# All low words of the expert weights on VectorE, and one buffer moved from the low words to the raw weights

## The chip, the cores and the metric

The kernel runs on one core of a Trainium2 chip. The metric is the device time of one execution in microseconds (us). Engines are named as in the profile: PE is the matrix engine, PEld its weight loads, DVE the vector engine, ACT the scalar engine, POOL is GpSimd, SP issues most of the DMAs. Each engine works through its own instructions in order and waits on semaphores for the others.

## What is computed

Attention with a sigmoid in place of the softmax, then a mixture of eight experts in which every token goes to one expert (greedily, by the largest gate values, 224 tokens to each expert), then a two-layer network on all tokens. Inputs and outputs are fp32.

```
attn = 1 / (1 + exp(-(q @ k.T / sqrt(64) - log(448))));  x = attn @ v      # 4 x 12 heads, 448 rows
for e in range(8):                                        # tokens assigned to e: 224 of 1792
    h = maximum(x[mask] @ w1[e], 0)                       # 768 -> 1024
    out[mask] = h @ w2[e]                                 # 1024 -> 768
r = maximum(out @ w_in, 0);  g = s * (r * r) + b          # 768 -> 2048
y = g @ w_out                                             # 2048 -> 768
```

## The kernel before

**Two words for each operand.** Every fp32 operand of a matmul is split in two: a high word `wh`, which ACT makes by a copy that rounds to fp32r (`w_high`, line 242), and a low word `wl`, the raw value minus the high word (`w_low`, line 252). A product is then three passes: high by high, high by low, low by high. In `half_mm` (lines 713 and 714) the two passes with the high weights are one matmul, with the high and the low half of the moving operand side by side (448 columns), and the third is a matmul of 224 columns with `wl`. `short_mm` (lines 731 to 733) does the same in three matmuls.

**Units.** Weights come in units of 128 x 768 words (384 KB). A unit is loaded into a buffer `raw` by a DMA on SP's queue (`w_dma`, line 218), ACT makes `wh` from it, DVE or POOL makes `wl`, and then the `raw` buffer is free for a later DMA. There are four `raw`, five `wh` and five `wl` buffers. SP issues the next load as soon as a `raw` buffer is free. The list `where` tells which low words POOL makes: of the 16 units of an expert, numbers 0, 2, 4, 6 and 12 (in expert 0 only 6 and 12), 37 in all. All other low words are DVE's. Four more, of the first units, are made on POOL at the end of the attention by `w_low(G)`, in both kernels.

**An expert** (`expert`) has two loops. The first has eight column groups, one unit each: six by `half_mm`, two by `short_mm`. After each, ACT copies half of the PSUM result (line 718), DVE adds it to the other half (line 719), and the result is rounded into `u` (ACT line 780, DVE line 781, or 736 behind `short_mm`). The second loop has six column groups `d` of eight 128-row blocks, so that each group uses one unit and a third; its results go into `y` (ACT 725, DVE 726) in experts 0 to 5, and into the operands of the mixing stage in experts 6 and 7 (DVE 823, 828, 835, 768, 770). In experts 0, 2, 4, 5 and 6 `x_split` brings in the next expert's rows during the first loop: three transposes on PE (704), a copy on ACT (706), a subtraction on DVE (707), four times.

**What sets the order.** All orders are written out by hand. `advance` is called inside `half_mm`, right behind the addition on line 719, and queues what the next units need: loads up to 8 units ahead, low words up to `use + ahead - 1`, high words up to `use + ahead`, where `use` is the number of units handed to PE so far and `ahead` is 5.

**The stages**, by the profile's clock: attention to about 165 us, the assignment of tokens to 204, experts 0 and 1 to 270, the first layer for them (`layer_in`) to 331, experts 2 and 3 to 396, `layer_in`, the second layer (`outputs`) to 544, experts 4 to 7 to 680, then the first layer in a form with seven half-size products in place of eight (`layer_mixed`), and `outputs` again. `outputs` scatters finished rows to DRAM by indirect DMAs on POOL's queue (`scatter`, line 853); the rows of an expert are fetched by two indirect DMAs on the same queue (`gather`, line 609).

Of the kernel before, what the change touches and what calls it, by code (L numbers as in the profile page):

```python
# [28 lines left out]
KD = DM // 128  # L29
KF = F1 // 128  # L30
# [33 lines left out]
def tile_kernel(ctx, tc, qT, kT, v, wg, w1, w2, wi, wo, s2, b2, cst, out):  # L64
# [1 line left out]
    V, A, G, T = nc.vector, nc.scalar, nc.gpsimd, nc.tensor  # L66

    const = ctx.enter_context(tc.tile_pool(name="const", bufs=1))
    wraw = ctx.enter_context(tc.tile_pool(name="wraw", bufs=4))
    wsp = ctx.enter_context(tc.tile_pool(name="wsp", bufs=5))  # L70
    wlp = ctx.enter_context(tc.tile_pool(name="wlp", bufs=5))
    xrp = ctx.enter_context(tc.tile_pool(name="xrp", bufs=2))
    dpool = ctx.enter_context(tc.tile_pool(name="dpool", bufs=1, space=DRAM))
    ctx.enter_context(tc.manual_schedule())
# [102 lines left out]
    units, where = [], []  # L177
    raws, splits, sums = {}, {}, {}
    nu = {"dma": 0, "pre": 0, "high": 0, "low": 0, "use": 0, "ahead": 5}
# [14 lines left out]
    for g in range(4):  # L194
        for e in (2 * g, 2 * g + 1):
            units += [w1[e, f] for f in range(KF)] + [w2[e, n] for n in range(KF)]
            where += [n in ((0, 2, 4, 6, 12) if e else (6, 12)) for n in range(2 * KF)]
        more = [narrow[f] for f in range(KG)] if g < 2 else []
        if g == 3:
            more = [(0, 1), (1, 1), (0, 2), (1, 2), (0, 3), (1, 3), (0, 4)]  # L200
            for f in range(2, KG // 2):
                more += [(f, 1), (f - 1, 4), (f, 2), (f, 3)]
            more += [(KG // 2 - 1, 4)]
        if g % 2:
            more += [w for of in products for w in of]
        units += more
        where += [False] * len(more)
# [38 lines left out]
    def w_low(eng=None):  # L246
        i = nu["low"]
        if i < nu["high"]:
            r, h = w_source(i), splits[i]
            lo = wlp.tile([128, KD, 128], F32R, name="wl")[:, :r.shape[1]]  # L250
            eng = eng or (G if where[i] else V)
            eng.tensor_sub(lo, r, h.bitcast(F32))  # L252
            splits[i] = (h, lo)
            nu["low"] += 1
# [304 lines left out]
    def full(pk):  # L559
        V.tensor_copy(flag, pk)  # L560
# [42 lines left out]
    def gather(e):  # L603
        if e >= E:
            return
        for h, n in enumerate(HT):
            if (e, h) not in xr:
                xr[e, h] = xrp.tile([128, DM], F32, name="xr")
            G.indirect_dma_start(out=xr[e, h][:n], out_offset=None, in_=xs,
                                 in_offset=bass.IndirectOffsetOnAxis(ap=idx[:n, h, e:e + 1], axis=0))  # L610
# [69 lines left out]
    def row_ids():  # L680
        def put(dst, rows, h, col, r0, n, src):
            for r in range(0, n, 32):
                G.tensor_copy(dst[rows + r:rows + r + 32, col], idx[r0 + r:r0 + r + 32, h, src])

        a, b = slice(0, E, 2), slice(1, E, 2)
        put(idt[:, 0], 0, 0, slice(0, 4), 64, 64, a)
        put(idt[:, 0], 64, 1, slice(0, 4), 0, 64, a)
        put(idt[:, 1], 0, 1, slice(0, 4), 64, 32, a)
        put(idt[:, 1], 32, 0, slice(0, 4), 0, 96, b)
        put(idt[:, 2], 0, 0, slice(0, 4), 96, 32, b)  # L690
        put(idt[:, 2], 32, 1, slice(0, 4), 0, 96, b)
        put(idl, 0, 0, slice(0, 2), 0, 64, slice(0, 4, 2))
        put(idl, 64, 0, slice(0, 2), 0, 64, slice(4, E, 2))
# [15 lines left out]
    def half_mm(weights, src, n, done, ahead, tt=None):  # L709
        p = ps_m.tile([128, 512], F32, name="acc")  # L710
        for k in range(n):
            wh, wl = weights(k)
            T.matmul(p[:, :2 * CAP], wh, src[:, k].rearrange("p a s -> p (a s)"), start=(k == 0), stop=False)  # L713
            T.matmul(p[:, :CAP], wl, src[:, k, 0], start=False, stop=(k == n - 1))  # L714
        t2 = pool["y"].tile([128, 2, CAP], F32, name="tmp", bufs=pool["tmp"])
        bs = t2[:, 0]
        tt = t2[:, 1] if tt is None else tt
        A.copy(bs, p[:, CAP:2 * CAP])  # L718
        V.tensor_add(tt, p[:, :CAP], bs)
        if ahead:  # L720
            advance()
        done(tt, bs)

    def two(dst, src):
# [13 lines left out]
    def w_dmas():  # L738
        while nu["dma"] < min(nu["use"] + 8, len(units)):
            w_dma()  # L740

    def w_lows():
        while nu["low"] < min(nu["use"] + nu["ahead"] - 1, nu["high"]):
            w_low()

    def w_highs():
# [2 lines left out]
                w_pre()  # L749
            w_high()  # L750

    def advance():
        w_dmas()
        w_lows()
        while nu["pre"] < min(nu["use"] + nu["ahead"] + 1, nu["dma"]):
            w_pre()
        w_highs()
# [16 lines left out]
    def expert(e, y):  # L774
        x = xg.pop(e)
        u = ml.tile([128, KF, 2, CAP], F32R, name="u")

        def first(f):
            def done(tt, _):
                A.activation(u[:, f, 0], tt, AF.Relu)  # L780
                V.scalar_tensor_tensor(u[:, f, 1], tt, 0.0, u[:, f, 0].bitcast(F32), op0=ALU.max, op1=ALU.subtract)  # L781

            return done

        for f in range(KF):
            wh, wl = w_get()
            if f < KF - 2:
                half_mm(lambda k: (wh[:, k], wl[:, k]), x, KD, first(f), f < KF - 3)
                if f == KF - 3:
                    advance()  # L790
            else:
                short_mm(wh, wl, x, KD, (u[:, f, 0], u[:, f, 1]))
                if f == KF - 2:
                    advance()
            if 1 <= f <= 4 and (e % 2 == 0 or e == 5):
                x_split(e + 1, f - 1)
            if f >= 1 and out_rows:
                scatter(*out_rows.pop(0))
        if e in (4, 5):
            gather(e + 2)  # L800
        sl = slice((e % 2) * CAP, (e % 2 + 1) * CAP)
        held = []
        if e == 6:
            mov["b22"] = m2p.tile([128, HK, 2, S], F32R, name="x")
        elif e == 7:
            mov["t3"] = m2p.tile([128, HK, 2, S], F32R, name="x")

        def halves(name, d, cols=sl):
            return mov[name][:, d, 0, cols], mov[name][:, d, 1, cols]

        for d in range(KD):
            def second(k):
                n, c = divmod(d * KF + k, KD)
                if n == len(held):
                    held.append(w_get())
                return [w[:, c] for w in held[n]]

            def done(tt, spare):
                if e < 6:
                    two((y[:, d, 0, sl], y[:, d, 1, sl]), tt)  # L820
                    return
                if d < HK:
                    V.tensor_sub(spare, tt, full(0, d, sl))
                    work = [(halves("t1", d), spare)]
                    if e == 7:
                        work.append((halves("t3", d, slice(0, CAP)), full(1, d, slice(0, CAP))))
                else:
                    V.tensor_sub(full(1, d - HK, sl), full(1, d - HK, sl), tt)
                    work = [(halves("b22", d - HK), tt)]
                    if e == 7:  # L830
                        work.append((halves("t3", d - HK), full(1, d - HK, sl)))
                for dst, src in work:
                    A.copy(dst[0], src)
                for dst, src in pending:
                    V.tensor_sub(dst[1], src, dst[0].bitcast(F32))
                pending[:] = work
                if e == 7 and d in (0, 1):
                    mix(2 - d, slice(0, CAP))

            tt = None  # L840
            if e in (4, 5):
                tt = full(d // HK * 2, d % HK, sl)
            elif e > 5 and d < HK:
                tt = full(1, d, sl)
            half_mm(second, u, KF, done, d < KD - 1, tt)
            if not e and d == 1:
                row_ids()
            if e == 1 and 2 <= d <= 4:
                late_do(f"a{d - 2}", 0)

# [111 lines left out]
    def ahead(st, n, more=()):  # L962
        def lows():
            while na["low"] < min(n + 3, na["high"]):
                a_low(st)

        def sums():
            while na["sum"] < min(n + 5, 28):
                a_sum(st)

        w_dmas()
        work, more = [w_lows, lows, sums], list(more)
        while work or more:
            for q in (work, more):
                if q:
                    q.pop(0)()
        w_highs()
        while na["high"] < min(n + 4, 28):
            a_high(st)
# [261 lines left out]
```

## Time and profile before

| | before |
|---|---|
| median of 3 runs | 916.81 us (915.82 to 917.8) |
| the profiled execution | 918.23 us |
| its span, first to last instruction | 916.4 us |
| mean granted clock of PE | 0.976 of full speed |
| busy share: PE, DVE, ACT, POOL | 96%, 72%, 57%, 14% |

The profile is of one execution. A busy PE is one with a matmul in its pipeline, not one at its peak. An idle engine costs nothing unless PE waits for it in the end.

### The profile page before, as it was taken

The numbers are of one execution on the slowest core, as the hardware profiler recorded it, in microseconds if no ns is written. First come the engines' busy times: TensorE is split into PE (matmuls) and PEld (weight loads), VectorE is DVE, ScalarE is ACT, GpSimd is POOL, SyncE is SP. The second block draws the span as 40 slices with busy tenths as digits, with TensorE's granted clock in tenths as the row PEclk, the third lists the DMA queues.
The fourth block names the chain that finished last, engine by engine and source line by source line (L and its number), as shares of the span: only waits on it lengthen the run. The fifth ranks groups of instructions, "written<-read, shape, count | busy, mean of one in ns | idle before, by whom it ended". The sixth has DMA issues, their size and how long they took to land.

```text
span 916.4 us, 14216 instructions
## 1 busy us (share of the span) xinstructions
PE 879.4 (96%) x5219; PEld 755.4 (82%) x5219; DVE 659.4 (72%) x1101; ACT 519.5 (57%) x895; POOL 130.0 (14%) x131
## 2 busy tenths in 40 slices
PE   9999999789999999999999999899997999999997
PEld 4554555559989989999999998898996899999997
DVE  3877885646678777689767855877897788768680
ACT  6666666736555565643565545666655455654540
POOL 1000003222600033300000035422300000000003
PEclk9999999769999999999999999999998999999999
DMA  9989994755768775759643438665541212332213
GB/s 291 332 289 350 313 325 163 214 168 164 220 210 287 246 253 177 228 178 324 218 141 123 128 123 278 201 206 174 193 138 52 69 53 69 104 120 94 97 35 138
DMA packets 70186, 171.52 MB, mean 187 GB/s; under 512 B 8160, under 2 KB 25056, under 8 KB 70112
## 3 DMA queue, kind: packets, MB, share of 16 engines
q1 hardware_dynamic: 67840, 159.56, 53.3%
q0 software_dynamic: 2272, 11.01, 3.4%
q8 instruction: 42, 0.69, 0.3%
q14 instruction: 32, 0.26, 0.1%
HBM read 142.23 MB, written 28.31 MB: 186 GB/s over the span
## 4 chain that ended last, share of the span: by engine, by line
PE 52%; DVE 9%; DMA 7%; issue 5%; ACT 3%; POOL 1%; POOLq 0%; ACTq 0%; DVEq 0%; SPq 0%
DMA raw<-in_w_dram 7%; PE acc L1014 6%; PE acc L1016 6%; PE acc L1017 6%; PE acc L860 4%; PE acc L861 4%; PE acc L862 4%; PE acc L713 4%; DVE wl L252 4%; PE acc L1108 3%; PE acc L1106 3%; PE acc L1107 3%; PE acc L714 2%; ACT wh L242 1%; DVE u L781 1%
## 5 line engine op out<-in xcount | busy, mean ns | idle before, releaser
L242 ACT CAST wh<-raw 128x768 fp32r<-128x768 f32 (+1 forms) x240 | 195.5, 823 | 119.5 <-issue 48.0
L252 DVE TENSOR_TENSOR wl<-raw,wh 128x768 fp32r<-128x768 f32 (+1 forms) x199 | 191.9, 971 | 45.4 <-ACT wh L242 45.0
L252 POOL TENSOR_TENSOR wl<-raw,wh 128x768 fp32r<-128x768 f32 x41 | 82.5, 2016 | 439.9 <-ACT wh L242 439.8
L713 PE MATMUL acc<-u,wh 128*128 128x448 f32 x384 | 122.9, 378 | 1.6 <-DVE u L736 1.3
L714 PE MATMUL acc<-u,wl 128*128 128x224 f32 x384 | 102.3, 266 | 2.5 <-DVE wl L252 2.5
L302 ACT ACTIVATE attn<-psc,nls 112x896 f32<-112x896 f32 x96 | 88.8, 1008 | 10.1 <-PE psc L300 10.1
L713 PE MATMUL acc<-x,wh 128*128 128x448 f32 x288 | 93.7, 380 | 0.6 <-issue 0.6
L713 PEld LDWEIGHTS acc<-u,wh 128*128 128x128 f32 x384 | 72.8, 189 | 8.4 <-DVE u L736 3.0
L714 PE MATMUL acc<-x,wl 128*128 128x224 f32 x288 | 76.6, 266 | 2.3 <-DVE wl L252 2.3
L311 PE MATMUL pv<-attn,vt 112*64 112x448 f32 x384 | 77.5, 546 | 0.0
L714 PEld LDWEIGHTS acc<-u,wl 128*128 128x128 f32 x384 | 74.1, 193 | 2.8 <-DVE wl L252 2.8
L860 PE MATMUL acc<-y,wh 128*128 128x448 f32 x192 | 71.2, 371 | 0.9 <-ACT y L725 0.9
L861 PE MATMUL acc<-y,wh 128*128 128x448 f32 x192 | 70.6, 368 | 0.0
L862 PE MATMUL acc<-y,wl 128*128 128x448 f32 x192 | 70.3, 366 | 0.0
L311 PEld LDWEIGHTS pv<-attn,vt 112*64 112x64 f32 x384 | 25.4, 136 | 43.0 <-issue 36.1
L714 PEld LDWEIGHTS acc<-x,wl 128*128 128x128 f32 x288 | 55.0, 191 | 3.4 <-DVE wl L252 3.4
L713 PEld LDWEIGHTS acc<-x,wh 128*128 128x128 f32 x288 | 54.1, 188 | 4.5 <-issue 0.8
L1014 PE MATMUL acc<-wh,as 128*128 128x384 f32 x168 | 56.3, 335 | 0.0
L1017 PE MATMUL acc<-wh,as 128*128 128x384 f32 x168 | 56.2, 334 | 0.0
L1016 PE MATMUL acc<-wl,as 128*128 128x384 f32 x168 | 56.1, 334 | 0.0
L718 ACT COPY tmp<-acc 128x224 f32<-128x224 f32 x96 | 32.6, 340 | 21.1 <-PE acc L714 20.4
L781 DVE SCALAR_TENSOR_TENSOR u<-tmp,u 128x224 fp32r<-128x224 f32 x48 | 30.6, 639 | 18.0 <-ACT u L780 18.0
(341 smaller groups left out, 2027.9 us busy)
## 6 DMA issues: line engine op xcount, KB each, us to landing
raw<-in_w_dram SPq DMA_DIRECT2D x128, 384.0 KB, 3.5
raw<-nw SPq DMA_DIRECT2D x72, 384.0 KB, 3.2
craw<-in_wi_dram SPq DMA_DIRECT2D x16, 768.0 KB, 6.1
raw<-mx SPq DMA_DIRECT2D x32, 384.0 KB, 2.9
nw<-co SPq DMA_DIRECT2D x24, 384.0 KB, 6.9
craw<-in_wo_dram SPq DMA_DIRECT2D x8, 768.0 KB, 5.6
ra<-in_wo_dram SPq DMA_DIRECT2D x8, 768.0 KB, 6.4
rqk<-in_kT_dram SPq DMA_DIRECT2D x24, 224.0 KB, 6.6
```

The lines of the kernel that those rows point to most:

```text
L242: A.copy(h, r)
L252: eng.tensor_sub(lo, r, h.bitcast(F32))
L302: A.activation(attn[n][:, :, c, :], p[:, :, :S], AF.Sigmoid, bias=nls[:CP], scale=1.0 / math.sqrt(D))
L311: T.matmul(pv[j * 64:(j + 1) * 64, :S], v[:, c, j * D:(j + 1) * D], a[:, j, c, :], start=(c == 0), stop=(c == NC - 1))
L713: T.matmul(p[:, :2 * CAP], wh, src[:, k].rearrange("p a s -> p (a s)"), start=(k == 0), stop=False)
L714: T.matmul(p[:, :CAP], wl, src[:, k, 0], start=False, stop=(k == n - 1))
L860: T.matmul(p, wh, src[:, k, 0], start=first, stop=False)
L861: T.matmul(p, wh, src[:, k, 1], start=False, stop=False)
L862: T.matmul(p, wl, src[:, k, 0], start=False, stop=last)
L1014: T.matmul(acc, hi, wh[:, cols], start=(opens[j] and u == 0 and c == 0), stop=False, skip_group_check=True)
L1016: T.matmul(acc, hi, wl[:, cols], start=False, stop=False, skip_group_check=True)
L1017: T.matmul(acc, lo, wh[:, cols], start=False, stop=(u == 3 and c == 1), skip_group_check=True)
```

## The change

The list `where` is all False, so every low word that POOL made is DVE's. `raw` has five buffers in place of four, `wl` four in place of five. Since a half-used unit holds its `wl` buffer in the second loop of an expert, low words are queued there one unit less far ahead (`w_lows(2)`: up to `use + ahead - 2`), as in `outputs`; elsewhere the distance is as before. The call that fetches the rows of expert 6 is moved from behind expert 4's first loop to behind the third group of its second.

```diff
-    wraw = ctx.enter_context(tc.tile_pool(name="wraw", bufs=4))
+    wraw = ctx.enter_context(tc.tile_pool(name="wraw", bufs=5))
-    wlp = ctx.enter_context(tc.tile_pool(name="wlp", bufs=5))
+    wlp = ctx.enter_context(tc.tile_pool(name="wlp", bufs=4))
...
-            where += [n in ((0, 2, 4, 6, 12) if e else (6, 12)) for n in range(2 * KF)]
+            where += [False] * (2 * KF)
...
         if ahead:
-            advance()
+            advance(ahead)
...
-    def w_lows():
-        while nu["low"] < min(nu["use"] + nu["ahead"] - 1, nu["high"]):
+    def w_lows(n=1):
+        while nu["low"] < min(nu["use"] + nu["ahead"] - n, nu["high"]):
...
-    def advance():
+    def advance(n=1):
         w_dmas()
-        w_lows()
+        w_lows(n)
...
-                half_mm(lambda k: (wh[:, k], wl[:, k]), x, KD, first(f), f < KF - 3)
+                half_mm(lambda k: (wh[:, k], wl[:, k]), x, KD, first(f), int(f < KF - 3))
...
-        if e in (4, 5):
-            gather(e + 2)
+        if e == 5:
+            gather(7)
...
-            half_mm(second, u, KF, done, d < KD - 1, tt)
+            half_mm(second, u, KF, done, 2 if d < KD - 1 else 0, tt)
...
+            if e == 4 and d == 2:
+                gather(6)
...
-        work, more = [w_lows, lows, sums], list(more)
+        work, more = [lambda: w_lows(2), lows, sums], list(more)
```

Three places show how the instructions stand. On DVE, where expert 0 passes into expert 1 (719 is the addition behind a group, 252 a low word, 726 ends a group of the second loop, 781 one of the first), before:

```order
L719 TENSOR_TENSOR tmp<-acc,tmp 128x224
L726 TENSOR_TENSOR y<-tmp,y 128x224
L719 TENSOR_TENSOR tmp<-acc,tmp 128x224
L252 TENSOR_TENSOR wl<-raw,wh 128x768
L781 SCALAR_TENSOR_TENSOR u<-tmp,u 128x224
L719 TENSOR_TENSOR tmp<-acc,tmp 128x224
L252 TENSOR_TENSOR wl<-raw,wh 128x768
L781 SCALAR_TENSOR_TENSOR u<-tmp,u 128x224
```

and in the changed kernel:

```order
L719 TENSOR_TENSOR tmp<-acc,tmp 128x224
L726 TENSOR_TENSOR y<-tmp,y 128x224
L719 TENSOR_TENSOR tmp<-acc,tmp 128x224
L252 TENSOR_TENSOR wl<-raw,wh 128x768 x2
L781 SCALAR_TENSOR_TENSOR u<-tmp,u 128x224
L719 TENSOR_TENSOR tmp<-acc,tmp 128x224
L252 TENSOR_TENSOR wl<-raw,wh 128x768 x2
L781 SCALAR_TENSOR_TENSOR u<-tmp,u 128x224
```

Behind each of the first two groups of an expert DVE now has two low words, the first of which is for the third group. On DVE, at the start of the mixing stage (1077 and 770 prepare moving operands, 1122 and 1123 finish the second product, `wl<-xr` is the low word of a unit that is a sum of two), before:

```order
L719 TENSOR_TENSOR tmp<-acc,tmp 128x224
L252 TENSOR_TENSOR wl<-raw,wh 128x768
L252 TENSOR_TENSOR wl<-xr,wh 128x768
L231 TENSOR_TENSOR raw<-raw 128x384
...
L770 TENSOR_TENSOR rb<-rb,ra 128x3x224
L1077 TENSOR_TENSOR u<-ra,u 128x3x448
L1122 TENSOR_TENSOR tmp<-acc,tmp 128x448
L1123 SCALAR_TENSOR_TENSOR tmp<-tmp 128x448
L252 TENSOR_TENSOR wl<-xr,wh 128x768
```

and in the changed kernel, whose lines from here on are numbered two higher:

```order
L719 TENSOR_TENSOR tmp<-acc,tmp 128x224
L252 TENSOR_TENSOR wl<-raw,wh 128x768
L231 TENSOR_TENSOR raw<-raw 128x384
...
L770 TENSOR_TENSOR rb<-rb,ra 128x3x224
L1079 TENSOR_TENSOR u<-ra,u 128x3x448
L252 TENSOR_TENSOR wl<-xr,wh 128x768
L1124 TENSOR_TENSOR tmp<-acc,tmp 128x448
L1125 SCALAR_TENSOR_TENSOR tmp<-tmp 128x448
L252 TENSOR_TENSOR wl<-xr,wh 128x768
```

The low word of the first sum, for the fifth product, has moved from ahead of the whole preparation to behind it. On POOL, from the last scatter of the first `outputs` to the first of the second, before:

```order
L853 DMA out_dram<-rb,idt 1792x768
L609 DMA xr<-xs,idx 128x768
L609 DMA xr<-xs,idx 96x768
L252 TENSOR_TENSOR wl<-raw,wh 128x768 x5
L609 DMA xr<-xs,idx 128x768
L609 DMA xr<-xs,idx 96x768
L252 TENSOR_TENSOR wl<-raw,wh 128x768 x11
```

and in the changed kernel:

```order
L855 DMA out_dram<-rb,idt 1792x768
L609 DMA xr<-xs,idx 128x768
L609 DMA xr<-xs,idx 96x768
L609 DMA xr<-xs,idx 128x768
L609 DMA xr<-xs,idx 96x768
```

The two fetches for expert 6 stand right behind the scatters in both; only the low words are gone. The order on PE, ACT and SP is unchanged.

## Rows read from the trace of the kernel before

**Rows 1.** The page's groups, line 252: count | busy us, mean ns | idle before
```profile
L252 DVE TENSOR_TENSOR wl<-raw,wh 128x768 fp32r<-128x768 f32 (+1 forms) x199 | 191.9, 971 | 45.4 <-ACT wh L242 45.0
L252 POOL TENSOR_TENSOR wl<-raw,wh 128x768 fp32r<-128x768 f32 x41 | 82.5, 2016 | 439.9 <-ACT wh L242 439.8
```
**Rows 2.** Windows, experts 0 to 7: length, busy PE, PEld, DVE, ACT, POOL, clock, DMA
```profile
204.55:237.14 32.59, 32.04 (x217) 30.32 (x217) 21.33 (x38) 20.33 (x43) 13.88 (x22) 1.00 0.58 181
237.14:269.76 32.62, 31.58 (x207) 29.30 (x205) 24.00 (x42) 19.94 (x42) 9.08 (x6) 1.00 0.70 223
331.14:363.48 32.34, 32.01 (x218) 30.20 (x216) 22.26 (x37) 20.59 (x44) 8.51 (x6) 1.00 0.68 219
363.48:396.40 32.92, 31.39 (x206) 29.22 (x205) 23.41 (x40) 20.07 (x44) 9.83 (x6) 1.00 0.67 214
544.37:580.05 35.68, 33.16 (x217) 31.58 (x217) 20.12 (x35) 20.20 (x43) 18.30 (x19) 0.95 0.72 236
580.05:614.44 34.39, 32.01 (x218) 30.30 (x217) 27.21 (x42) 22.27 (x47) 13.63 (x8) 1.00 0.65 208
614.44:648.06 33.62, 31.75 (x219) 30.30 (x217) 27.13 (x45) 19.51 (x43) 8.63 (x5) 1.00 0.59 183
648.06:680.05 31.99, 30.87 (x206) 29.14 (x205) 27.75 (x48) 20.43 (x45) 8.22 (x5) 1.00 0.59 192
```
**Rows 3.** Timeline of PE in expert 0's first loop: start us, us, instruction
```profile
205.24 0.38 PE L713 MATMUL acc<-x,wh 128*128 128x448 f32 x1
...
205.87 0.37 PE L713 MATMUL acc<-x,wh 128*128 128x448 f32 x1
...
218.08 0.27 PE L731 MATMUL acc<-x,wh 128*128 128x224 f32 x1
...
219.09 0.27 PE L731 MATMUL acc<-x,wh 128*128 128x224 f32 x1
```
**Rows 4.** Waits of PE, 204 to 700 us: us in total, times, longest
```profile
PE acc L1108 <- DVE wl L252: 5.2, 1, 5.2
PE acc L714 <- DVE wl L252: 4.8, 4, 2.5
PE px L704 <- DVE x L707: 4.4, 4, 1.9
```
**Rows 5.** Timeline of DVE and POOL at 209, 243 and 622 us
```profile
209.43 3.46 DVE L252 TENSOR_TENSOR wl<-raw,wh 128x768 fp32r<-128x768 f32 x2
...
243.79 0.38 DVE L719 TENSOR_TENSOR tmp<-acc,tmp 128x224 f32<-128x224 f32 x1
...
622.07 1.82 POOL L252 TENSOR_TENSOR wl<-raw,wh 128x768 fp32r<-128x768 f32 x1 [1.71 <-ACT wh L242]
622.31 1.82 DVE L781 SCALAR_TENSOR_TENSOR u<-tmp,u 128x224 fp32r<-128x224 f32 x1 [0.54 <-ACT u L780]
```
**Rows 6.** Line 781 alone: duration ns min/median/max, first and last start
```profile
L781 DVE SCALAR_TENSOR_TENSOR u<-tmp,u x48: 376/392/2037, 208.8 to 664.2; 128x224 fp32r<-128x224 f32 x48
```
**Rows 7.** Timeline of DVE, POOL and ACT between 532 and 571 us
```profile
532.56 0.55 DVE L1031 TENSOR_TENSOR rb<-acc,rb 128x384 f32<-128x384 f32 x1
...
547.90 1.23 POOL L853 DMA_INDIRECT out_dram<-ra,idt  x1 [0.17 <-issue]
...
570.39 0.83 ACT L242 CAST wh<-raw 128x768 fp32r<-128x768 f32 x1 [2.94 <-DMA raw<-in_w_dram]
```
**Rows 8.** Timeline of DVE from expert 7's second loop into the mixing stage
```profile
669.33 2.04 DVE L823 TENSOR_TENSOR tmp<-ra 128x224 f32<-128x224 f32 x1
...
690.12 1.56 DVE L1077 TENSOR_TENSOR u<-ra,u 128x1344 fp32r<-128x1344 f32 x1
693.49 0.62 DVE L1122 TENSOR_TENSOR tmp<-acc,tmp 128x448 f32<-128x448 f32 x1 [1.81 <-ACT tmp L1113]
...
694.69 0.95 DVE L252 TENSOR_TENSOR wl<-xr,wh 128x768 fp32r<-128x768 f32 x1
```
**Rows 9.** Window at the start of the mixing stage, columns as in rows 2
```profile
692.20:699.00 6.80, 3.30 (x9) 2.96 (x10) 4.80 (x8) 4.10 (x7) 0.00 (x0) 0.50 0.00 0
```

## The prediction, made before the changed kernel was run

> **What bounds the kernel now.** I read the busy shares in the table first: PE is busy for 96% of the span, DVE for 72%. So the change can give back only what PE loses to waits. Which stages lose is seen in the windows of the eight experts, the stages for whose weights POOL makes low words [rows 2]. What an expert would take without waits follows from the spacing of the matmuls: two pairs of half_mm start 0.63 us apart, so a pair costs 0.315 us, and nine short matmuls take 1.01 us, so one costs 0.112 [rows 3]. An expert has 6 x 6 + 6 x 8 = 84 pairs and 36 short ones: 26.5 + 4.0 = 30.5 us. The windows with about 218 matmuls where the others have 206 hold twelve transposes more; at an estimated 0.09 us each, somewhat under the wider short ones, these take 1.1 us, so 31.6 us. Against that the windows lose, experts 0 to 7: 1.0, 2.1, 0.7, 2.4, 4.1, 2.8, 2.0 and 1.5 us, together 16.6 us. Then comes the start of the mixing stage, where PE waits once for 5.2 us.
>
> Next, what PE waits for [rows 4]: low words from DVE, and transposed rows (x, line 707) from DVE. Yet DVE is busy for only 56 to 87% of these windows [rows 2]. The timeline tells why [rows 5]: at 622.07 POOL starts a low word, 1.82 us long; 0.24 us later DVE starts line 781, which has 224 columns and a median of 0.392 us [rows 6], and takes 1.82 us. It is released as POOL ends. Every DVE instruction from 200 to 680 us that takes well over its own usual time runs beside a POOL low word: 31 of them, the first in the pair at 209.43 (3.46 us for two) [rows 5], the last at 669.33 (2.04 us for 224 columns, which take 0.38 elsewhere [rows 5]) [rows 8]; their excess sums to 39.2 us. Line 719, which takes one input from PSUM, is not among them. So a POOL low word does not relieve DVE; it holds it, and with it the ACT and PE work behind it in order.
>
> The Trainium skill speaks for and against the edit here (Perfetto Trace Analysis, section Optimizing Scalar/DVE Operations): with DVE saturated, offloading even to GPSIMD may make sense, but as the two share a read port it might not help. The 1.82 us of line 781 [rows 5] agree with the second half. By the first half alone, the added low words would come on top of DVE's busy time.
>
> **The change part by part.** *Low words to DVE.* Added: 37 at 0.97 us, the mean on DVE [rows 1], 36 us of DVE time. Removed: the 39.2 us of holding. Net -3 us, so DVE is not fuller than now. Even if no holding were given back, expert 7, with the fullest DVE, would go from 27.75 to 27.75 + 5 x 0.97 = 32.6 us in a window of 32.0; with the 5.0 us of holding of its four held instructions (the last is that at 669.33) given back, it comes out at its present 27.6. Expert 0 is the model: there DVE made 14 of 16 low words already, and it lost 1.0 us, part of it behind its own POOL word at 209.43. I take it that 0.4 us per expert remains: 16.6 - 8 x 0.4 = **13.4 us gained**. The bounds: nothing remains (16.6), or all lose what expert 0 loses (16.6 - 8.0 = 8.6).
>
> *Where the longest losses go.* Expert 4 loses most: ACT waits 2.94 us for a raw weight at 570.39 [rows 7], PE behind it, and then runs some 3.6 us at the lower clock (the window's mean of 0.95 [rows 2] is 3.6 of 35.68 us at half). The loads are slow there because six scatters and two fetches run from 547.90 on [rows 7]. Three of these rows are finished at 533.1, when DVE ends the last of its three additions [rows 7]; their scatters stand behind POOL low words. With those gone they can start some 14 us earlier, beside lighter traffic, and the raw weights of expert 4 meet half the crowd.
>
> *Five raw buffers, four low.* In the first loop a load starts one unit earlier, 6 x 0.315 = 1.9 us of cover. In the second loop low words are queued one unit later, so the load starts where it did: no gain, no loss. PE is covered against the later low word: at most one unit and a third of a group of 8 x 0.315 = 2.5 us ahead of use, more than the 0.97 us it takes. Priced at nothing; if that cover fails, it is the third rival.
>
> *The third unit of an expert* now has its low word queued behind the first group, in the five places where an expert follows another. It must be ready 1.9 us later; addition 0.38 [rows 5] + low word 0.97, behind an ACT copy of the same 224 columns that I put at 0.35, is 1.7. This is tight: bounds 0 to 1.2 us a place (4.8 us over four such waits of line 714 [rows 4]); I take 0.2, inside the 0.4 above.
>
> *Start of the mixing stage.* The hold at 669.33 goes: 2.04 - 0.38 = 1.66 us off a DVE chain that is busy almost without a gap to 690.12 + 1.56 = 691.7 [rows 8]. But the low word for the fifth product, now behind that chain, ends at 691.7 - 1.66 + 0.95 = 691.0, and PE reaches it at about 687.8 (680.05, the end of expert 7's window, and 38 matmuls of 448 columns at 0.315 - 0.112 = 0.203): a new wait of 3 us. The word for the sixth product waits on ACT (the 1.81 us of idle time at 693.49 [rows 8] take up the inserted word), so it ends at 695.6 - 1.66 = 694.0. PE goes on there between 694.0 and, if the fifth product runs at the lower clock, 694.7, in place of 695.7: 1.0 to 1.7 us. After the old wait PE ran 3.30 busy us at 0.50 of its clock [rows 9], at 1.2 GHz in place of 2.4, a loss of 1.65; some of it falls into the shorter waits now. I take **2.0 us**, bounds 0 and 3.3.
>
> *The moved fetch.* Priced at nothing: POOL's order has the two fetches behind the scatters in both kernels. As POOL's low words are gone, all fetches start as soon as their buffer is free, earlier than now, not later. Two fetches of 0.7 MB together may collide with weights in experts 0 and 2; the spare 1.9 us of the fifth buffer covers that.
>
> Sum: 13.4 + 2.0 = 15.4 us off 918.23, the profiled execution, gives 902.8. That execution lies 1.4 us over the median, so **901.4**, put as 901.5.
>
> **The rivals.** (1) *All waits go.* The upper bounds, 16.6 + 3.3 = 19.9: 916.8 - 19.9 = 896.9, and less if the stages behind the experts start smoother too. For: all these waits end on DVE [rows 4]. Against: in a chain so strictly in order some other wait comes last.
> (2) *DVE as the bound.* The holding is given back, but the pairs of low words at an expert's start arrive as bursts on an engine that is 79 to 87% busy in experts 5 to 7 [rows 2]; half the gain, 8 us: 909. For: line 714 waits on DVE four times [rows 4], with fewer low words on it than after the change. By the first half of the Trainium skill's sentence (Perfetto Trace Analysis, Optimizing Scalar/DVE Operations) the time would come out here or later.
> (3) *Slower: the late low word.* If DVE comes to the third unit's word 2.5 us late, the longest wait of line 714 [rows 4], PE stops and then runs at the lower clock for 3.6 us as in expert 4: 2.5 + 1.8 = 4.3 us at five places, 21.5 us, more than the 15.4 gained: 916.8 - 15.4 + 21.5 = 922.9. It decides from 3.1 us a place. For: the word has only 0.2 us to spare. Against: nothing is queued between the addition and it, and a lag of DVE has the POOL holds as its main cause.
> (4) *It does not do what it says*: if the scatters still crowd expert 4, its 4.1 us stay: 905.5, inside the range.
>
> **How the numbers follow.** Forecast 901.5, with 897 to 907 (case 4 in it), 0.60; all waits go, 890 to 897, 0.12; DVE as the bound, 907 to 913, 0.18; within 0.2% (1.8 us, about what a measurement of this kernel can tell from no change) 0.04; slower 0.06. Faster: 0.60 + 0.12 + 0.18 = 0.90. The range leaves out the lower half of case 1, the upper part of case 2 and both signs beyond: 894 to 910.
>
> **What would show it.** Right: no DVE instruction of experts 0 to 7 over twice its median; DVE's busy time about as before (656 us); experts of 30.5 to 32.5 us, expert 4 without a low clock; the first scatters at 531 to 534 us; PE waiting about 3 us for the low word of the fifth product at the start of the mixing stage. Wrong: long DVE instructions without POOL beside them; waits on line 714 in the third group of experts 1, 3, 5, 6 or 7; ACT still waiting 2 us and more for raw weights in the second loops.

## The result, and the profile after

The changed kernel takes **895.19 us** (median of 4 runs, 894.83 to 897.01), the kernel before 917.3 in the same session: a ratio of 0.9763, 95% interval 0.9742 to 0.9784. The forecast was 901.5 us, "faster", with a range of 894 to 910. The time lies in the range, but the experiments show that most of the gain came from an edit that the prediction priced at nothing. The profiled execution took 897.01 us, 21.2 less than that of before (918.23). Line numbers behind line 848 are two higher than in the kernel before.

From the page of the changed kernel: busy time, the clock, and the groups of lines 242 and 252 (busy us, mean ns | idle before).
```profile
PE 871.6 (97%) x5219; PEld 754.9 (84%) x5219; DVE 655.5 (73%) x1138; ACT 521.9 (58%) x895; POOL 52.6 (6%) x94
PEclk9999999859999999999999999999999999999999
L242 ACT CAST wh<-raw 128x768 fp32r<-128x768 f32 (+1 forms) x240 | 194.8, 823 | 88.3 <-issue 68.0
L252 DVE TENSOR_TENSOR wl<-raw,wh 128x768 fp32r<-128x768 f32 (+1 forms) x236 | 218.3, 937 | 15.3 <-PE acc L1018 11.3
```
Beside [rows 1], DVE made 37 low words more and its mean fell from 971 to 937 ns; its total busy time went from 659.4 to 655.5 us, so the net of -3 us that the prediction worked out came about. Its idle time in front of low words for want of a high word from ACT, 45 us in [rows 1], is down to 0.7. So ACT, too, comes earlier. That is the first hint at what the prediction missed.

The experts 0, 1, 4 to 7 and the mixing stage of the changed kernel as windows (columns as in [rows 2]).
```profile
203.59:238.83 35.24, 33.41 (x216) 31.81 (x217) 23.00 (x44) 20.94 (x44) 6.63 (x20) 0.95 0.59 200
238.83:269.18 30.35, 30.35 (x206) 29.17 (x205) 23.69 (x44) 20.55 (x42) 0.00 (x0) 1.00 0.64 212
537.65:569.16 31.51, 31.51 (x217) 30.33 (x217) 22.49 (x42) 21.39 (x45) 3.95 (x5) 1.00 0.70 231
569.16:600.69 31.53, 31.53 (x219) 30.34 (x217) 24.56 (x47) 21.67 (x47) 2.10 (x3) 1.00 0.70 222
600.69:632.21 31.52, 31.52 (x218) 30.34 (x217) 24.68 (x48) 21.65 (x46) 0.00 (x0) 1.00 0.64 195
632.21:662.99 30.78, 30.63 (x207) 29.18 (x205) 25.65 (x51) 18.60 (x40) 0.00 (x0) 1.00 0.62 198
662.99:772.50 109.51, 104.79 (x507) 95.80 (x506) 88.09 (x143) 60.19 (x98) 0.00 (x0) 0.98 0.20 64
```
In experts 1 and 4 to 6 PE is busy for the whole window, as in experts 2 and 3 (not shown): the windows are within 0.2 us of the 30.5 and 31.6 us that the prediction worked out for an expert without waits. Expert 0 alone got longer, 35.24 against 32.59 in [rows 2].

Waits of PE in the changed kernel between 200 and 720 us (us in total, times, longest), in place of [rows 4].
```profile
PE acc L1110 <- DVE wl L252: 3.1, 1, 3.1
PE px L704 <- DMA xr<-xs,idx: 1.8, 1, 1.8
PE acc L1108 <- ACT rb L1115: 1.7, 1, 1.7
```
The second is in expert 0: the fetched rows of expert 1 land late, and the clock is at 0.50 for 3.4 us behind that wait (from 209.70 us). The first is the start of the mixing stage. By stages, in profiled time: the eight experts went from 266.2 to 252.8 us (13.4 less), the mixing stage from 113.7 to 109.5 (4.2), and what lies before, between and behind them from 538.3 (that is 918.23 - 266.2 - 113.7) to 534.7, some 3.6 us less.

### The profile page after: what moved, and what is told of

Same layout as the page of the kernel before. It is cut to its first block, busy times and chain, and to the rows that moved or that the text cites. A ratio compares the mean times of both kernels' runs of the same rounds, so it can differ in the third digit from the quotient of the medians.

```text
span 895.1 us, 14131 instructions
## 1 busy us (share of the span) xinstructions
PE 871.6 (97%) x5219; PEld 754.9 (84%) x5219; DVE 655.5 (73%) x1138; ACT 521.9 (58%) x895; POOL 52.6 (6%) x94
## 4 chain that ended last, share of the span: by engine, by line
PE 71%; DVE 3%; issue 1%; DMA 1%; ACT 1%; POOL 0%; POOLq 0%; ACTq 0%; DVEq 0%
PE acc L713 15%; PE acc L714 7%; PE acc L1019 6%; PE acc L1016 6%; PE acc L1018 6%; PE acc L862 4%; PE acc L864 4%; PE acc L863 4%; PE acc L1110 3%; PE acc L1108 3%; PE acc L1109 3%; PE acc L732 1%; PE acc L731 1%; PE acc L733 1%; PE px L704 1%
## 5 line engine op out<-in xcount | busy, mean ns | idle before, releaser
L252 DVE TENSOR_TENSOR wl<-raw,wh 128x768 fp32r<-128x768 f32 (+1 forms) x236 | 218.3, 937 | 15.3 <-PE acc L1018 11.3
L713 PE MATMUL acc<-u,wh 128*128 128x448 f32 x384 | 120.8, 374 | 0.0
L719 DVE TENSOR_TENSOR tmp<-acc,tmp 128x224 f32<-128x224 f32 x78 | 30.1, 386 | 29.3 <-ACT tmp L718 28.9
L281 DVE CAST wh<-rqk 128x896 fp32r<-128x896 f32 x22 | 13.8, 626 | 36.4 <-DMA rqk<-in_qT_dram 36.4
```

## The experiments

The change has three parts that can be set one by one: who makes the 37 low words (DVE or POOL), the number of raw buffers (4 or 5), and how late a low word is queued (old or new order). The new order comes with four low-word buffers and the later fetch of expert 6 in runs 2, 5 and 6; run 7 has the later fetch and four low-word buffers with the old order. No run has five buffers of each kind. All ratios are against the kernel before in the same session (median 917.3 us in that of the result, 918.5 to 918.8 in the others). "ACT waits" is the idle time of ACT in front of high words that ended with the landing of a raw weight of an expert; "DVE held" sums, over the DVE instructions from 195 to 870 us, what each takes over its own usual time.

| kernel | low words | raw, low buffers | order | median us | ratio (95%) | ACT waits, us | DVE held, us |
|---|---|---|---|---|---|---|---|
| before | POOL | 4, 5 | old | 918.5 to 918.8 | 1 | 33.8 | 39.2 |
| 1 | DVE | 4, 5 | old | 914.6 | 0.9946 (0.9916-0.9976) | 39.2 | 0 |
| 6 | POOL | 4, 4 | new | 919.7 | 1.0011 (0.9983-1.0038) | 37.1 | 30.6 |
| 5 | DVE | 4, 4 | new | 914.3 | 0.9940 (0.9913-0.9967) | 49.9 | 0 |
| 2 | POOL | 5, 4 | new | 903.0 | 0.9826 (0.9770-0.9882) | 10.1 | 34.0 |
| after (run 9) | DVE | 5, 4 | new | 897.6 | 0.9776 (0.9753-0.9799) | 5.1 | 0 |

(The last two columns of the last line are from the profiled execution shown above.)

**1. Low words on DVE alone.**
```
-            where += [n in ((0, 2, 4, 6, 12) if e else (6, 12)) for n in range(2 * KF)]
+            where += [False] * (2 * KF)
```


> All 37 low words of GpSimd go to DVE, while the buffers (four raw, five low-word), the order at the end of an expert and the place of the fetches stay as before. Theory A (a two-input instruction of POOL holds DVE, and this alone cost the experts their time): the whole difference of the changed kernel comes from here, 895 to 899 us, no DVE instruction of an expert over twice its median, expert windows of 30.3 to 31.6 us. Rival D (the fifth raw buffer or the low words queued later carry part of it): 903 to 912 us, with ACT waiting for raw weights in front of its high words.

Measured: 914.64 us, a gain of 0.5%. Theory A as it was put has fallen: no DVE instruction is held any more, and yet three quarters of the gain (1.8 of 2.4%) are missing.

**2. Buffers and order alone.** The changed kernel with the line above put back.


> The changed kernel with the 37 low words put back on GpSimd: five raw and four low-word buffers, the later queueing of the last low word and the later fetch remain. Theory A: 914 to 919 us, as the kernel before, with DVE instructions of 1.8 to 2.1 us in the experts again; the mixing at the end keeps its new wait of 3 us and loses only what the hold at its start cost. Rival D (the buffers carry the gain): 900 to 910 us.

Measured: 902.96 us, 1.7% under before, although DVE is held for 34 us as in the kernel before. So the larger part comes with the buffers, the order and the later fetch together; runs 5 and 6 tell these apart. What they did is seen in what ended ACT's idle time in front of its high words (line 242; us, times). The kernel before:
```profile
L242 ACT CAST wh<-raw x240: 492/836/849, 144.3 to 889.7; 128x768 fp32r<-128x768 f32 x116, 128x384 fp32r<-128x384 f32 x4
  DMA raw<-in_w_dram: 33.8, 26
```
run 1:
```profile
  DMA raw<-in_w_dram: 39.2, 37
```
run 2:
```profile
  DMA raw<-in_w_dram: 10.1, 9
```
and the changed kernel:
```profile
  DMA raw<-in_w_dram: 5.1, 11
```
In the kernel before ACT waited 26 times for a raw weight, 33.8 us in all, 20.7 of it while PE was in a second loop. The prediction read one of these waits (570.39, [rows 7]) and blamed a crowd of transfers for it; the other 25 have no part in it.

**5. The changed kernel with four raw buffers,** the one-line test of that.
```
-    wraw = ctx.enter_context(tc.tile_pool(name="wraw", bufs=5))
+    wraw = ctx.enter_context(tc.tile_pool(name="wraw", bufs=4))
```


> The changed kernel with four raw buffers in place of five; low words on DVE, four low-word buffers and the new order remain. Theory R (the fifth raw buffer carries the larger part, since ACT's high words wait for raw weights without it): 910 to 916 us, ACT waiting 35 to 40 us for raw weights, as in the run with the low words on DVE alone. Theory O (the order carries it: low words queued a unit later in the second loop and in the merging of the outputs): 895 to 900 us.

Measured: 914.29 us, and ACT's waits as theory R has them or above:
```profile
  DMA raw<-in_w_dram: 49.9, 47
  DMA raw<-nw: 15.0, 13
```
Theory R stands: this one buffer is worth some 914.3 - 897.6 = 16.7 us (run 9 is the changed kernel in another session; 15 us by the two ratios). How run 5 loses them is seen in its timeline in the second loop of expert 5 (start us, us, engine):
```profile
602.88 1.80 SPq L218 DMA_DIRECT2D raw<-in_w_dram  x2
603.04 0.39 DVE L719 TENSOR_TENSOR ra<-acc,tmp 128x224 f32<-128x224 f32 x1
603.34 0.95 DVE L252 TENSOR_TENSOR wl<-raw,wh 128x768 fp32r<-128x768 f32 x1
605.23 0.84 ACT L242 CAST wh<-raw 128x768 fp32r<-128x768 f32 x1 [2.50 <-DMA raw<-in_w_dram]
605.97 0.38 ACT L725 CAST y<-ra 128x224 fp32r<-128x224 f32 x1
606.25 0.34 ACT L718 COPY tmp<-acc 128x224 f32<-128x224 f32 x1
606.37 0.39 DVE L726 TENSOR_TENSOR y<-ra,y 128x224 fp32r<-128x224 f32 x1 [2.08 <-ACT y L725]
```
ACT stands for 2.50 us before the high word of 605.23 until its raw weight has landed. Behind it wait ACT's copies for y, and behind those DVE, idle for 2.08 us. PE still has work here; it stops for 0.8 us at 615.02, for a low word, and for 1.2 us at 620.37, for rows that DVE makes. The chain of work that ended last leads from here to the second of these waits (its pieces, start us and us; those between are left out):
```profile
603.42 0.88 DVE wl L252
604.30 0.02 SPq L218
604.36 3.77 DMA raw<-in_w_dram
608.97 0.38 ACT y L725
609.38 0.39 DVE y L726
610.07 0.88 DVE wl L252
611.00 4.30 DMA raw<-in_w_dram
617.17 1.75 DVE wl L252 x2
619.78 0.54 DVE x L707
620.37 0.47 PE px L704 x3
```
It is a ring: a low word frees a raw buffer, SP issues the next load into it, ACT waits for that load, DVE for ACT, and the next low word for DVE. DVE's waits and PE's waits are the end of this chain, and they carry DVE's name. Of the chain through the whole execution such loads are 61.6 us in the kernel before, 63.3 in run 1, 55.1 in run 5 and 50.0 in run 6, but 13.4 in run 2 and nothing in the changed kernel.

**6. The new order with POOL's low words and four raw buffers.** Run 5 with the line of run 1 put back.


> The kernel before with only the new order, its four low-word buffers and the later fetch; 37 low words on GpSimd and four raw buffers stay. Theory R: 914 to 920 us, ACT waiting about 34 us for raw weights as before. Theory O: 901 to 906 us, as in the run with buffers and order together.

Measured: 919.71 us, the same as before within the interval; ACT waits 37.1 us. Theory O has fallen: the new order, with four low-word buffers and the later fetch, gives nothing as long as there are four raw buffers. With it the parts can be added up from medians: the raw buffer 919.7 - 903.0 = 16.7 us with POOL's low words and 16.7 with DVE's; the move of the low words 919.7 - 914.3 = 5.4 us with four raw buffers and 903.0 - 897.6 = 5.4 with five. That they agree to a tenth is luck: only one of the four pairs (919.7 and 914.3) ran in one session, and by the ratios it is 17.0 and 15.1 us for the buffer, 6.5 and 4.6 for the move. Within this noise the two gains add. The intervals part the 16.7 clearly from nothing; the 5.4 is clear with four buffers (0.9913-0.9967 against 0.9983-1.0038), while with five the two intervals overlap.

**3. Dummy subtractions on POOL,** in the changed kernel, after each of the 37 low words of DVE; the result is not used.
```
+            if spots[i]:
+                hf = h.bitcast(F32)
+                for s in (slice(0, HK), slice(HK, r.shape[1])):
+                    G.tensor_sub(scr[:, :s.stop - s.start], hf[:, s], hf[:, s])
```


> The changed kernel with dummy work on GpSimd: at each of the 37 places where it made a low word, it now subtracts the high word from itself, in two halves of 384 columns, into a scratch tile that nobody reads; the low words stay on DVE. Theory A (POOL's two-input work holds DVE): DVE instructions of 1 to 2 us stand in the experts again, 15 to 40 us of excess in all, and the time goes up to 903 to 918 us. Rival B (what cost the time was that a low word made on POOL is ready a microsecond later than one made on DVE): nothing waits for the scratch, so 895 to 898 us.

Measured: 907.81 us, ratio 0.9859 (0.9816-0.9903), some 10 us over run 9 by the medians and 8 by the ratios; 32.8 us of holding. The timeline at expert 6 (its line numbers in these functions are three to nine higher):
```profile
611.96 2.45 DVE L255 TENSOR_TENSOR wl<-raw,wh 128x768 fp32r<-128x768 f32 x2
612.49 2.60 POOL L259 TENSOR_TENSOR scr<-wh 128x384 bf16<-128x384 f32 x2 [3.46 <-ACT wh L245]
614.33 1.01 DVE L788 SCALAR_TENSOR_TENSOR u<-tmp,u 128x224 fp32r<-128x224 f32 x1
```
Two low words take 2.45 us in place of 1.87, and line 788 (781 in the kernel before) 1.01 in place of 0.39 [rows 6]. Nobody reads the scratch, so rival B is out: the holding itself is real and costs time, 8 to 10 us for 32.8 us of it. What failed was the price put on taking it away.

**4. Dummy copies on POOL,** the same with `G.tensor_copy(scr[:, :s.stop - s.start], hf[:, s])`.


> As the run with the dummy subtractions, but each of the 37 places copies the high word into the scratch tile, in two halves of 384 columns: one input in place of two. Theory A in its narrow form (only a two-input instruction of POOL holds DVE): 895 to 898 us and no long DVE instruction. In its wide form (any work of POOL on SBUF holds DVE): 903 to 918 us, as with the subtractions.

Measured: 898.50 us, ratio 0.9776 (0.9737-0.9815), that of the changed kernel. These copies read the same high words at the same places as the subtractions of run 3, which speaks against the rival that run 3 only held the buffers of the high words for longer. The narrow form holds for the time, but not to the letter:
```profile
634.87 2.12 DVE L255 TENSOR_TENSOR wl<-raw,wh 128x768 fp32r<-128x768 f32 x2
635.39 1.97 POOL L259 CAST scr<-wh 128x384 bf16<-128x384 f32 x2 [3.84 <-ACT wh L245]
636.91 0.69 DVE L788 SCALAR_TENSOR_TENSOR u<-tmp,u 128x224 fp32r<-128x224 f32 x1
```
Line 788 still takes 0.30 us more than usual, and no DVE instruction of this run takes over 0.32 more; 10.8 us in all. The copies themselves take 0.51 us alone and up to 1.30 beside DVE's two-input instructions.

**7. The changed kernel with the old order.**
```
-            half_mm(second, u, KF, done, 2 if d < KD - 1 else 0, tt)
+            half_mm(second, u, KF, done, int(d < KD - 1), tt)
-        work, more = [lambda: w_lows(2), lows, sums], list(more)
+        work, more = [w_lows, lows, sums], list(more)
```


> The changed kernel with the order of before: low words queued up to one unit short of the high words in the second loop and in the merging of the outputs too. Five raw buffers and the low words on DVE remain. Theory R: 894 to 899 us. Theory O: 908 to 916 us, DVE waiting at the ends of the experts for a low-word buffer.

Measured: 909.60 us, ratio 0.9897 (0.9862-0.9933). The time is that of theory O, but the place is not. The experts take 250.3 us, no more than in the changed kernel; the loss is behind them: 151.2 us against 147.0 from expert 3 to expert 4, 114.8 against 109.5 in the mixing stage, 127.7 against 122.6 behind it. The group of DVE's low words on the page of run 7, and two of its waits of PE from 200 to 860 us:
```profile
L252 DVE TENSOR_TENSOR wl<-raw,wh 128x768 fp32r<-128x768 f32 (+1 forms) x236 | 218.8, 939 | 57.9 <-issue 43.4
```
```profile
PE acc L1110 <- DVE wl L252: 5.2, 1, 5.2
PE acc L1016 <- DVE ra L1033: 4.7, 4, 1.5
```
DVE stands idle for 57.9 us ahead of low words, 15.3 in the changed kernel, nearly all of it while the outputs are merged (450 to 541 us, and from 775 us on), and PE waits there for additions (line 1033) that are queued behind. My reading is that with four buffers a low word queued early waits for the oldest buffer and holds up DVE. For it speaks that between 450 and 541 us 23 of the 24 low words with idle time before them start 0.09 us behind the end of a matmul of line 1018 that reads a low word; the page names no releaser for 43.4 us of it, so it is argued. Shown is that with four low-word buffers and five raw ones the new order is worth some 12 us (1.2% by the ratios), though it was worth nothing inside the experts.

**8 and 10. The remaining wait at the start of the mixing stage.** One low word more queued ahead of the mixing's preparation, and then two:
```
-            half_mm(second, u, KF, done, 2 if d < KD - 1 else 0, tt)
+            half_mm(second, u, KF, done, 2 if d < KD - 1 or e == 7 else 0, tt)
```


> The changed kernel with one low word more queued ahead behind the last product of expert 7, so that the low word of the fifth product of the mixing stands on DVE ahead of the preparation of the mixing. If that wait (3.2 us at 670.5 in the changed kernel) is this place in DVE's queue alone: 892 us, no wait of TensorE for a low word there over 0.5 us. If the preparation that is now late is waited for next: 894 to 896 us, the wait at another instruction of the same stretch.

Measured: 899.68 us, ratio 0.9799 (0.9756-0.9843): no gain. The fifth product's word is ready at 667.5 us now, and PE waits 5.2 us for the next one, made at 675.58:
```profile
666.52 0.95 DVE L252 TENSOR_TENSOR wl<-xr,wh 128x768 fp32r<-128x768 f32 x1
675.58 0.95 DVE L252 TENSOR_TENSOR wl<-xr,wh 128x768 fp32r<-128x768 f32 x1
```
For both words the argument of that line is `2 if d < KD - 1 else int(e == 7)`; the changed kernel ran beside it.


> The changed kernel itself once more, unaltered, beside the run after it: 895 to 899 us, as the base that the next one is read against, since the kernels before it ran in other sessions.

Measured: 897.56 us, ratio 0.9776 (0.9753-0.9799).


> The changed kernel with two low words more queued behind the last product of expert 7, so that those of the fifth and of the sixth product of the mixing both stand on DVE ahead of its preparation (with one alone the wait moved to the sixth and grew to 5.4 us). If place in DVE's queue is all: 3 us under the unaltered kernel of the same call, no wait of TensorE over 1 us for a low word between 660 and 680 us. If the preparation, now 2.5 us later on DVE, is waited for instead: within 1.5 us of it, with the wait at the first product that reads the preparation's output.

Measured: 898.56 us, ratio 0.9778 (0.9754-0.9803): the same. The waits of PE in run 10 between 655 and 720 us:
```profile
PE acc L1108 <- ACT tmp L1115: 3.2, 3, 1.6
PE acc L1108 <- ACT rb L1115: 2.0, 1, 2.0
PE acc L1109 <- DVE x L1077: 0.5, 1, 0.5
```
No wait for a low word is left, and 3.2 us of waits for ACT's copies stand in its place: these stand on ACT behind the conversion of the preparation's output (line 1081), which waits for DVE, as ACT's timeline has it:
```profile
672.82 1.31 ACT L1081 CAST ra<-rb 128x1344 fp32r<-128x1344 f32 x1 [1.63 <-DVE u L1079]
674.04 0.53 ACT L1115 COPY tmp<-acc 128x448 f32<-128x448 f32 x1
```
In each of these three orders PE stops in this stretch, for one of two low words or behind the preparation. None of these kernels beats the changed one.

## Why the prediction was right, and where its reasons were wrong

**The total.** Forecast 15.4 us of gain, measured 21.2 in the profiled executions. The experts gave 13.4, the very number forecast, which is luck, as it is a sum of other parts: experts 1 to 7 gained 16.0, all of their waits, and expert 0 lost 2.7. The median of 895.19 us lies in the band of the first rival (890 to 897, with the stages behind the experts "smoother too"), which had a chance of 0.12, and not in the 897 to 907 that had 0.60.

**"Five raw buffers, four low: priced at nothing"** is the step that failed. It said that in the second loop low words are queued one unit later, so that the load starts where it did. Measured over the 64 units of the second loops, from the issue of a raw load on SP to PE's first matmul with that unit: 10.6 us in the kernel before and 10.5 in run 5 (four raw buffers, old and new order), 13.1 in the changed kernel and 13.2 in run 7 (five, new and old). The order moves nothing; the buffer moves the load by 2.5 us, one column group of 8 x 0.315. The low word was not held back by its place in DVE's queue but by its high word, and this by its load. The sum that was due, an estimate from these rows: an expert has 16 units in 31.5 us, 1.97 us each, so four buffers give every unit 7.9 us for its load, its high word and its low word. These take 3.5 us (the page's median from issue to landing, before) + 0.84 + 0.95 = 5.3 us, and 2.6 us is left for standing in line behind other work on two engines that run in order. Five buffers leave 4.5 us.

**"Low words to DVE: 13.4 us".** The mechanism was right, and run 3 shows it: a two-input subtraction on POOL holds DVE's two-input instructions. Its price was wrong by the factor 13.4 / 5.4: the move, which gives back 39.2 us of held DVE time and adds 36 us of low words, is worth some 5 us. (The 8 to 10 us of run 3 are for holding alone, with the low words on DVE as well.) In the experts alone it is 4.1 us from before to run 1, 6.6 from run 6 to run 5 and 5.1 from run 2 to the changed kernel, one profiled execution each. The prediction put down to DVE every wait of PE that ended on DVE. The timeline of run 5 shows why that does not follow: DVE was waiting for ACT, and ACT for a load.

The Trainium skill (SBUF — State Buffer, section Who interferes with whom) has it that a DVE instruction with two SBUF inputs contends with a GpSimd instruction that reads SBUF, and that contention is for a shared port pair, as an exclusive lock. Runs 2 and 3 agree for two-input work on POOL. In run 4 one-input copies contend too, but copies with a median of 0.78 us cost a DVE instruction 0.3 us at most.

**Expert 4** lost 4.1 us and loses nothing now, but the reason given was one of two. In run 2 the scatters stood behind POOL's low words as in [rows 7], from 541.56 us on, and expert 4 still took 31.51 us:
```profile
537.26:568.77 31.51, 31.51 (x217) 30.32 (x217) 19.65 (x35) 20.15 (x43) 18.54 (x19) 1.00 0.82 278
```
In run 1, with four raw buffers, the scatters came early and it took 31.50. Either cures it. In run 6, with neither, it took 32.1 us and not the 35.7 of [rows 2]; whether the rest of that loss was one execution's, or went with the new order and the later fetch, no run tells. That the scatters would come earlier was right: the first is at 524.79, 12.9 us ahead of expert 4, where it was 3.5 us behind its start.

**The mixing stage.** The new wait of about 3 us for the fifth product's low word came as forecast (3.1, start at 670.50). Two terms were off. The hold at 669.33, priced at 1.66 us, was worth nothing: run 1 has no hold and the old wait of 5.2 us; run 2 has POOL's low words and the new one of 3.1. And the gain was 4.2 us, above the bound of 3.3, for the prediction counted the clock at one place only. Windows of the kernel before:
```profile
680.05:793.77 113.72, 106.34 (x506) 96.91 (x505) 88.44 (x144) 60.29 (x98) 0.00 (x0) 0.95 0.19 60
722.90:726.30 3.40, 3.40 (x10) 3.02 (x11) 1.54 (x3) 1.04 (x2) 0.00 (x0) 0.50 0.37 116
```
and of the changed kernel:
```profile
673.90:677.30 3.40, 3.39 (x9) 3.04 (x10) 2.47 (x4) 2.05 (x4) 0.00 (x0) 0.50 0.00 0
703.00:707.00 4.00, 4.00 (x20) 3.72 (x21) 3.02 (x6) 1.70 (x3) 0.00 (x0) 1.00 0.35 98
```
Before, PE worked 3.3 us at 0.50 of the clock behind the first wait [rows 9] and again 3.4 us at 722.90, behind a second wait of 1.9 us that the prediction didn't list. Now it works 3.4 us at 0.50 behind the first wait, so nothing of the 1.65 us came back there, and at the full clock behind the second wait (1.7 us). PE's busy time for the same matmuls fell from 106.34 to 104.79, its idle time from 7.4 to 4.7.

**Not in the sum:** the 3.6 us outside the experts and the mixing stage. With four raw buffers (run 5) the stage behind expert 1 took 61.6 us and the one behind expert 3 148.0; in the changed kernel 59.6 and 147.0. So 2.8 us of it go with the raw buffer again: it serves those stages' weights too (raw<-nw, 15.0 us of waits in run 5). Another 1.0 us lies before expert 0, where the start differs by 2 us from run to run.

**The other rivals.** DVE as the bound did not come: no DVE instruction is held, and no low word of an expert is waited for by more than 0.3 us. The late low word did not come either: no wait on line 714 in the third groups. **The moved fetch** of expert 6 was not run by itself; PE waits for none of its rows, as said. But PE waits 1.8 us for the fetch for expert 1, which was not moved. It was issued 1.0 us earlier than before (202.94 and 204.22 us) and landed 0.6 to 0.7 us later (209.94, against 209.30); what slowed it is not shown. The prediction had thought of a collision in expert 0 only as a risk to the weights, covered by "the spare 1.9 us of the fifth buffer". That buffer holds weights and could not cover rows. In run 9 this wait was 1.3 us and expert 0 took 33.1 us.

## What to carry to other kernels

Price a ring of buffers by the time that one buffer is occupied (load, every reader, and their places in line), against the ring's length times the time per unit; in the experts here, how early its release was queued said nothing. Before blaming an engine for the waits that end on it, read what ended that engine's own idle time, back to the first that waits for nothing but a transfer: here one line, 33.8 us of ACT waiting for raw weights, pointed at the term that was put at nothing. And when a change has several parts, write down the gain of each alone before adding: a forecast of the sum can be right with its main terms wrong.

## What the runs showed of the hardware

A subtraction with two SBUF inputs on GpSimd stretched DVE's two-input instructions to about its own end (0.39 to 1.8-2.0 us, the kernel before), and pairs of such subtractions of 384 columns by at most 1.1 us (run 3); one-input copies of 384 columns, 0.5 to 1.3 us long, stretched them by 0.3 us and no more (run 4). 32.8 us of holding cost the changed kernel 8 to 10 us (run 3), and moving the low words off POOL, which ended 39 us of it and gave DVE 36 us of work, gained some 5 us.
